# The expert program of a fused attention and MoE kernel starts one attention step sooner, and its 32-token unit moves from ninth to fifth place

## The chip, the cores and the metric

The kernel runs on one core of a Trainium2 chip. The metric is the device time of one execution in microseconds. The kernel before takes 522.33 us, the median of three runs (521.17, 522.33 and 524.80).

TensorE (PE) multiplies and turns matrices; VectorE (DVE) and ScalarE (ACT) work on elements; GpSimd (POOL) issues the indirect DMAs; SyncE (SP) issues the plain DMAs and the transposing ones.

## The reference

Block-sparse attention, then a mixture of experts with one expert per token (top 1):

```
batch, heads, seq, dim = 4, 8, 768, 64        # attention
scores = q @ k^T / sqrt(64), masked to neighbour blocks of 32, the first and last block,
         and 3 sampled blocks for each block
x = softmax(scores) @ v                       # as 3072 tokens x 512
logits = x @ w_gate                           # 512 x 8
e = argmax(logits); gate = softmax(logits)[e]; eom = sigmoid(x @ w_output_gate)[e]
out = gate * eom * (relu(x @ w1[e]) @ w2[e])  # w1: 512 x 1024, w2: 1024 x 512, of 8 experts
```

## The kernel before, in words

**Attention** runs in 52 steps (`NSTEP`), two halves of the batch by 4 dense and 22 sparse ones. A step's parts go by name: `pS` multiplies q and k into a PSUM tile S, `dM` takes the row maximum (DVE, L506), `aE` the exps (ACT, L514), `pT` turns the probabilities (PE L463, copies L466 on ACT and L468 on DVE), `pO` multiplies by v (L531, L542) and `fin` divides. The parts of three steps are interleaved.

**Routing** goes along in hooks, `at(step, rank, function)`: `turn` turns a tile of 128 tokens (xp, L622, copied at L628), `route_p` multiplies by the gate weights (lp, L638), `route_s`, `route_a`, `route_r` (rp, L681 to L684) and `route_c` find each token's expert and its place among that expert's tokens. `route_d` scatters the tokens into a table `rows` in HBM, sorted by expert (POOL, L752). When the last tokens are counted, a plan is worked out (`plan`: some 45 small DVE operations, from L770 to L831, with one matmul `lb` on the tile `left` at L824). It gives the places `place_u` from which POOL then gathers x of every expert unit but the first (L896). The first unit, "unit 0", takes 512 tokens that are known to belong to one expert before the attention ends; it is turned on PE (xe, L911) and split on ACT and DVE (L915, L916).

**The experts** work in 13 units of tokens by 8 pieces of FF, numbered as steps 0 to 103 of the expert program. A piece is 512 KB of weights that SP loads (`load_w`, L887) into one of 14 buffers. As the products are in two halves of f16, ACT writes the high half of a piece (`w_h`, L970), DVE the low half (`w_l`, L974). Step s is a product h (12 matmuls, L996; h0, h1 ... in order), the relu and its split on ACT (`h_h`, L1005) and DVE (`h_l`, L1011); four steps later (`YL`) the product y follows (L1031). When a unit's y is complete, ACT scales it (`y_o`, L1041) and POOL scatters it to the output (`store_y`, L1049). x of a unit is gathered in `load_x`, split by `x_s` on ACT (L935) and DVE (L936), and turned by SP's transposing DMAs (`x_t`, L945). Unit 1 (`PEX`) is turned on PE instead (xgp, L953), and split by ACT L955 and DVE L956.

**What sets the order.** Each engine works in the order in which instructions are emitted. `program()` gives every expert instruction a step and a rank in it with `do(step, rank, f, a)`. `PACE` says which of the first expert steps are emitted at the end of the attention steps from `FIRST` = 51 on, `PLAN` and `PLAN0` where the planner's parts stand, `LW` and `WW` the first steps for weight loads and splits, `LEAD` (7) how many steps ahead of its product a piece is split. `WALK` gives the order of the units. Units hold, in that order, 512, 256, 352, 256, 288, 256, 256, 256, 256, 32, 192, 160 and 32 tokens. PSUM has banks of the pools psS (S tiles, large turns, two of a unit's y), psT (turned probabilities, h) and psO (O, a unit's third y); `late` in the route functions takes one of psS, otherwise psO.

Of the kernel before, what the change touches and what calls it, by code (L numbers as in the profile page):

```python
# [34 lines left out]
NRAW = 14  # L35
# [3 lines left out]
NPU, NIF = 4, 9  # L39
NR = len(CAPS)  # L40
PS = NPU + NR + NIF
IFS = (2, 3, 4)
WALK = [0, 4, 1, 5, 2, 6, 3, 7, 10, 8, 9, 11] + list(range(NPU + NR, PS))


def widths(c):

    return [128] * (c // 4) + ([32 * (c % 4)] if c % 4 else [])


SHAPE = [[128] * EM] + [widths(CAPS[w - NPU] if NPU <= w < NPU + NR else 8) for w in WALK]
MT = 3
# [8 lines left out]
LEAD = 7  # L61
# [15 lines left out]
FIRST = 51  # L77

WPRE = 44, 48, 52, 52, 53, 53, 54, 54
PACE = -1, -1, 1, 1, 2, 3  # L80

PLAN = 2, 3, 4
PLAN0 = 4
LW, WW = 4, 6

PH = {}
PEX = (1,)
XT = {1: 6}
XE = 51, 52
XG = 42, 43, 44, 45  # L90

# [36 lines left out]
def tile_kernel(ctx, tc, q, k, v, sampled, wg, wcat, out):  # L128
# [724 lines left out]
    NP = NUNIT * NFC  # L853
    toks = [sum(sh) for sh in SHAPE]
    per = [2 if t <= 256 else 1 for t in toks]

    def load_t(u):
        if u:
            assert len(scattered) == NT
        src = es[WALK[u - 1]:WALK[u - 1] + 1, 0:1] if u else eai  # L860
        _, r = nc.values_load_multi_w_load_instructions(src, engines=[ET.SP], min_val=0, max_val=E - 1)
# [31 lines left out]
    def gather_x(u, x, m):  # L893
        place_ = place_u[:, WALK[u - 1], m:m + 1] if u else place_0[:, m:m + 1]
        n = NT if u else RG[GE][1]
        i = nc.gpsimd.indirect_dma_start(  # L896
            x.bitcast(I32), None, rows, bass.IndirectOffsetOnAxis(ap=place_, axis=0)).ins
        after_scatters(i, n)
        if not u:
            tc.declare_no_dep(i, group="table", reason="rows of first tiles", keep=kept[:n])  # L900
            tc.add_to_no_dep_group("table", i)
# [81 lines left out]
    def bank_of(n):  # L983
        return n - n % per[n // 8]
# [82 lines left out]
    def at(n, rank, f, *a):  # L1067

        hooks.setdefault((n, rank), []).append((f, a))
# [36 lines left out]
    for bp in range(2):  # L1106
        o = PER * bp
        for r in range(RK):
            at(o + r if bp or not r else r + 2, 3, fixed, bp, r)
        if bp:  # L1110
            for r in range(RC):
                at(o + 2, 3, fixed_v, bp, r)
        for i in range(NPAIR):
            u0 = o + ND + 2 * i
            if bp or i > 1:
                at(u0 - 6, 1, load_q, bp, i)
            at(u0 - 3 if bp or i else u0 - 1, 3 if bp or i else 0, scale_q, bp, i)
            for kind, n, ns in KC:
                at(u0 - n, 3, gather_k, bp, i, kind, ns)
            at(u0 - 2, 3, window_k, bp, i)  # L1120
            if bp or i:
                at(u0 - 2, 1, window_v, bp, i)
            at(u0 - 1, 1, gather_v, bp, i, 0)
            at(u0, 1, gather_v, bp, i, 1)
        tiles = [NPAIR] + list(range(NPAIR))
        for n, i in enumerate(tiles):
            tt = 12 * bp + n

            r = o + ND + 1 + (2 * i + 2 if n else 0)
            at(r + 1, 2, turn, tt, r + 1 >= LATE_T, "act" if r + 1 < LATE_T else "dve")  # L1130
            at(r + 2, 0, route_p, tt, r + 2 >= LATE_T)
            at(r + 2, 1, route_s, tt)
            for g, (a, e) in enumerate(RG):
                if e == tt + 1:
                    t0 = r + 2
                    if e == NT:
                        at(t0, 3, part, route_a, 20, g)
                        at(t0 + 1, 0, route_r, g, True)
                        at(t0 + 1, 0, route_b, g)
                        at(t0 + 1, 1, mixed, g)  # L1140
                        for t in range(a, e):
                            at(t0 + 1, 3, route_d, t)
                        continue
                    if e == RG[-2][1]:
                        at(t0 + 1, 3, part, route_a, 20, g)
                        at(t0 + 2, 3, route_r, g, True)
                        at(t0 + 2, 3, route_b, g)
                        at(t0 + 2, 3, part, route_c, 20, g)
                        for t in range(a, e):
                            at(t0 + 2, 3, route_d, t)  # L1150
                        continue
                    for m, n_ in enumerate(PARTS[0]):
                        at(t0 + m, 3, part, route_a, n_, g)
                    at(t0 + 3, 0, route_r, g, t0 + 3 >= LATE_T)
                    at(t0 + 3, 0, route_b, g)
                    for m, n_ in enumerate(PARTS[1]):
                        at(t0 + 3 + m, 1, part, route_c, n_, g)
                    for t in range(a, e):
                        at(t0 + 5 + (t - a) * (1 if g else 2), 3, route_d, t)
                    if g == GE:  # L1160
                        for m in range(5):
                            at(t0 + 4 + m, 3, part, choose, 4, g)
                        at(t0 + 9, 3, load_t, 0)
# [3 lines left out]
        at(n, 3, turn_early, 2 * m)  # L1167
    for n in range(2):
        at(50 + 2 * n, 3, w_h, n)
        at(50 + 2 * n, 3, w_l, n)  # L1170
    for j, s in enumerate(WPRE):
        at(s, 3, load_w, j)

    done = set()

    def program(n0, n1):

        prog = {}

        def do(step, rank, f, a, hi=n1):  # L1180
            u = NFC if f in (load_w, w_h, w_l, p_h, p_y, h_h, h_l) else 1
            if n0 * u <= a < hi * u and (f, a) not in done:
                done.add((f, a))
                prog.setdefault(step, []).append((rank, len(prog[step]) if step in prog else 0, f, a))

        for i in range(3):
            do(PLAN[i], 8.5 if i == 2 else 12.5, plan, i)
        for u in range(NUNIT):
            t = 8 * u
            if u:  # L1190
                do(max(t - 20, LW), 0, load_t, u)
                do(max(t - 16, PLAN[2]), 8.6, load_x, u)
                do(max(t - (12 if u > 2 else 8), WW), 13, x_s, u)
            do(max(t - 6, WW if u else 0), 13, keep_t, u)
            do(XT.get(u, max(t - (11 if u > 2 else 6), WW)), 15, x_t, u)
            do(t + 8 + YL - (not u), 9.5 if not u else 12, y_o, u)
            do(t + 8 + YL + 1, 13, store_y, u)
        for n in range(NP):
            w = max(n - LEAD, WW + (n - 8) // 2) if n >= 8 else max(n - 2, 1)
            do(w, 12, w_h, n)  # L1200
            do(w, 12, w_l, n)
            if n >= 8:
                do(max(n - NRAW - LEAD + 1, LW + (n - 8) // 3), 14, load_w, n)
            do(PH.get(n, n), 8, p_h, n)
            do(n + YL, 9, p_y, n)
            b = per[n // 8]
            if n % b == b - 1:
                do(n + (n != 1), 10 if n != 1 else 16, h_h, bank_of(n))
                do(n + (n != 1), 11 if n != 1 else 16, h_l, bank_of(n))
        return prog  # L1210

    def emit(prog, upto):
        for step in sorted(k for k in prog if k < upto):
            for _, _, f, a in sorted(prog.pop(step), key=lambda z: z[:2]):
                if f is load_w and 10 <= a < NRAW + 8:
                    paced(tc, ET.SP, f, (a,))
                else:
                    f(a)


    done.update([(x_t, 0), (w_h, 0), (w_h, 1), (w_l, 0), (w_l, 1)])
    main = program(0, NSURE)

    def unit(n):
# [11 lines left out]
    for step in range(max(s for s, _ in hooks) + 1):  # L1236
# [45 lines left out]
        if step >= FIRST:  # L1282
            emit(main, PACE[step - FIRST])
    emit(main, 10 ** 6)
# [3 lines left out]
    def rest(n, k):  # L1288
        with tc.If(more > n):
            emit(program(1 + NR + n, 1 + NR + n + IFS[k]), 10 ** 6)  # L1290
            in_order(tc)
            if k + 1 < len(IFS):
                rest(n + IFS[k], k + 1)
# [63 lines left out]
```

## Time and profile before

| | |
|---|---|
| median of three runs | 522.33 us (521.17 to 524.80) |
| profiled execution | 522.23 us, its span 520.4 us |
| mean granted PE clock | 0.985 |
| busy: PE, DVE, ACT, POOL | 494.6 (95%), 347.7 (67%), 314.2 (60%), 231.3 us (44%) |
| HBM | 112.06 MB read, 12.85 MB written |

Times in the trace run from the start of the span. Attention and routing end, and the experts begin, between about 226 and 255 us. A number in brackets behind a row of a timeline is the time for which the engine was idle before it, with what ended that.

### The profile page before, as it was taken

What the parts mean: (1) busy time and instruction counts of PE and PEld (TensorE: products, weight loads), DVE (VectorE), ACT (ScalarE), POOL (GpSimd) and SP (SyncE); (2) the same over time, 40 slices, a digit from 0 to 9 for tenths busy, and PEclk for the clock granted to TensorE, in tenths of its full rate; (3) what the DMA queues carried; (4) which work ended last, traced back from release to release, by engine and by line L of the source; (5) the groups of instructions that cost most, each with busy time, mean ns of one, the idle gap of its engine ahead of it and who ended that gap; (6) DMA issues with size and microseconds to landing.
All of it is one profiled execution on the core that took longest, in us unless ns stands there. A gap on an engine that the chain in (4) does not pass through costs nothing.

```text
span 520.4 us, 18358 instructions
## 1 busy us (share of the span) xinstructions
PE 494.6 (95%) x7405; PEld 337.6 (65%) x7405; DVE 347.7 (67%) x683; ACT 314.2 (60%) x558; POOL 231.3 (44%) x411
## 2 busy tenths in 40 slices
PE   8999999999999999988899999999999999997994
PEld 7767777776677677764346655666566666665662
DVE  5776678656878687668858555464656656668770
ACT  3566777665657677664346746365465656667661
POOL 7575565570458768714440616050323304336222
PEclk9999999999989999999999999999999999997998
DMA  7977788694978879839499999989969899799501
GB/s 293 302 246 231 239 269 283 212 304 155 247 213 260 273 223 291 257 120 293 170 379 354 339 321 379 270 206 327 256 224 243 286 283 275 230 353 309 154 30 37
DMA packets 59902, 131.88 MB, mean 253 GB/s; under 512 B 28320, under 2 KB 28448, under 8 KB 59810
## 3 DMA queue, kind: packets, MB, share of 16 engines
q1 hardware_dynamic: 47314, 86.84, 55.9%
q0 software_dynamic: 12496, 43.79, 25.5%
q8 instruction: 60, 0.98, 0.8%
q14 instruction: 32, 0.26, 0.2%
HBM read 112.06 MB, written 12.85 MB: 240 GB/s over the span
## 4 chain that ended last, share of the span: by engine, by line
PE 75%; issue 7%; DMA 5%; DVE 4%; POOL 4%; POOLq 2%; ACT 2%; ACTq 0%; DVEq 0%
PE y L1031 25%; PE h L996 24%; PE S L499 7%; PE T L463 6%; PE O L542 4%; PE O L531 4%; DMA vt<-in_v_dram,vidx 3%; PE xp L622 2%; PE lp L638 2%; POOLq L424 2%; POOL kr L433 1%; DVE kr L974 1%; DMA vq<-in_v_dram 1%; DMA r<-in_wcat_dram 1%; DMA raw<-in_sampled_dram 1%
## 5 line engine op out<-in xcount | busy, mean ns | idle before, releaser
L974 DVE SCALAR_TENSOR_TENSOR kr<-r,kr 128x1024 f16<-128x1024 f32 x80 | 97.3, 1223 | 59.0 <-ACT kr L970 58.9
L1031 PE MATMUL y<-kr,hh 128*128 128x512 f16 (+3 forms) x759 | 110.7, 313 | 0.0
L970 ACT ACTIVATE kr<-r 128x1024 f16<-128x1024 f32 x80 | 84.0, 1057 | 40.1 <-PE y L1031 39.7
L1049 POOL DMA_INDIRECT out_dram<-yo,tab x28 | 34.7, 1241 | 165.0 <-ACT yo L1041 160.5
L996 PEld LDWEIGHTS <-kr 128*128 128x128 f16 x960 | 78.1, 98 | 36.9 <-issue 5.8
L1031 PEld LDWEIGHTS <-hh 128*128 128x128 f16 (+3 forms) x984 | 61.4, 98 | 58.4 <-issue 11.1
L996 PE MATMUL h<-xall,kr 128*128 128x256 f16 (+5 forms) x864 | 90.2, 252 | 3.4 <-DVE hh L1011 3.4
L514 ACT ACTIVATE P<-S,mx 128x256 f32<-128x256 f32 x176 | 69.7, 492 | 6.8 <-DVE mx L506 6.8
L448 POOL DMA_INDIRECT vt<-in_v_dram,vidx x44 | 43.3, 984 | 64.5 <-PE O L542 43.1
L506 DVE TENSOR_REDUCE mx<-S 128x4 f32<-128x1024 f32 x44 | 53.7, 1221 | 25.5 <-PE S L499 13.1
L1005 ACT ACTIVATE hh<-h 128x512 f16<-128x512 f32 (+5 forms) x64 | 31.5, 493 | 49.2 <-PE y L1031 27.3
L433 POOL COPY kr<-kn 128x256 f32 x132 | 48.6, 409 | 9.7 <-issue 8.3
L466 ACT COPY pt<-T 128x512 f32<-128x512 f32 x66 | 36.7, 592 | 25.7 <-PE T L463 25.7
L499 PE MATMUL S<-kr,qall 64*32 64x256 f32 x1408 | 50.5, 383 | 1.5 <-issue 1.5
L463 PE MATMUL T<-ident,P 128*128 128x128 f32 x352 | 48.3, 280 | 0.3 <-issue 0.3
L1011 DVE SCALAR_TENSOR_TENSOR hh<-h,hh 128x512 f16<-128x512 f32 (+5 forms) x64 | 35.5, 555 | 17.8 <-ACT hh L1005 17.8
L974 DVE SCALAR_TENSOR_TENSOR wx<-r,wx 128x1024 f16<-128x1024 f32 x24 | 29.3, 1226 | 18.9 <-ACT wx L970 18.9
L463 PEld LDWEIGHTS T<-ident,P 128*128 128x128 f32 x352 | 39.5, 143 | 3.2 <-issue 0.6
L896 POOL DMA_INDIRECT xb<-rows,place_u x24 | 32.9, 1370 | 12.0 <-issue 5.8
L996 PE MATMUL h<-xall,wx 128*128 128x256 f16 (+4 forms) x288 | 36.5, 279 | 0.0
L1031 PE MATMUL y<-wx,hh 128*128 128x512 f16 (+3 forms) x225 | 36.1, 321 | 0.0
L752 POOL DMA_INDIRECT rows<-xall,place x24 | 25.0, 1043 | 22.3 <-DVE xall L714 15.2
(271 smaller groups left out, 691.0 us busy)
## 6 DMA issues: line engine op xcount, KB each, us to landing
r<-in_wcat_dram SPq DMA_DIRECT2D x104, 512.0 KB, 5.7
vq<-in_v_dram SPq DMA_DIRECT2D x8, 780.0 KB, 4.8
qall<-in_q_dram SPq DMA_DIRECT2D x24, 256.0 KB, 5.2
vcall<-in_v_dram SPq DMA_DIRECT2D x22, 260.0 KB, 4.0
kn<-in_k_dram SPq DMA_DIRECT2D x10, 384.0 KB, 5.6
kn<-in_k_dram SPq DMA_DIRECT2D x3, 768.0 KB, 8.5
vcall<-in_v_dram SPq DMA_DIRECT2D x12, 130.0 KB, 10.5
vt<-in_v_dram,vidx POOLq DMA_INDIRECT x44, 6.2
```

Source lines behind the costliest of these rows:

```text
L433: nc.gpsimd.tensor_copy(r[:, slot], kn[bp][:, :, ds(rv, 1)].rearrange("p u o n -> p u (o n)"))
L448: nc.gpsimd.indirect_dma_start(vt[bp, i][:, s].rearrange("p b j w -> p (b j w)"), None, v, bass.IndirectOffsetOnAxis(ap=vidx[:, bp, i, s:s ...
L463: nc.tensor.transpose(pt[:, 128 * c:128 * c + 128], p[:, 128 * c:128 * c + 128], ident)
L466: nc.scalar.copy(t[:, 0:w], pt[:, 0:w])
L499: nc.tensor.matmul(s[64 * b + 32 * qi:64 * b + 32 * qi + 32, h2, hp], t[p, 64 * j + 32 * qi:64 * j + 32 * qi + 32], g[p, 1 - qi:3:1 + qi, ...
L506: nc.vector.tensor_reduce(mx, self.s.rearrange("p b h n -> p (b h) n"), axis=AX.X, op=ALU.max, negate=True)
L514: nc.scalar.activation(p[:, 256 * hp:256 * hp + 256], self.s[:, b, hp], AF.Exp, bias=self.mx[:, 2 * b + hp:2 * b + hp + 1])
L970: nc.scalar.activation(w[:, 0, r], piece(n // 8, n % 8)[:, r], AF.Copy, scale=SW)
L974: nc.vector.scalar_tensor_tensor(w[:, 1, r], piece(n // 8, n % 8)[:, r], SW, w[:, 0, r], op0=ALU.mult, op1=ALU.subtract)
L996: nc.tensor.matmul(hps[g][:, cols(n)], w[:, hl, 128 * c:128 * c + 128], x[:, xl, c, 0:t], start=cnt == 0, stop=cnt == 11)
L1011: nc.vector.scalar_tensor_tensor(hl[:, k], hps.pop(g)[:, k], 0.0, hh[:, k], op0=ALU.max, op1=ALU.subtract)
L1031: nc.tensor.matmul(y[t * p:t * p + t, 0:d], a[:, k:k + t], w[:, l, 512 + d * p:512 + d * p + d], start=n % 8 == 0 and cnt == 0, stop=n % 8 ...
```

## The change

Five things, of which none changes what is computed.

- `WALK`: the unit of 32 tokens that stood ninth stands fifth. Units now hold 512, 256, 352, 256, 288, 32, 256, 256, 256, 256, 192, 160 and 32 tokens.
- `PACE`, `PLAN`, `LW`, the step of `load_t` and `XT`: the expert steps 1 and on are emitted one attention step sooner; the plan, the loads of weights and of x keep their places by standing one expert step later. x of unit 1 is turned behind h7, between two products, rather than behind y2.
- `route_r` of the last group but one takes a bank of psO.
- The low split of piece 0 is emitted at step 51, behind the row maximum.
- `split_steps` gives the step at which each piece is split: instead of seven steps ahead throughout, it adds up for each step the time that its product takes against that of one split, puts splits off where steps are too short for them, and catches up. The loads follow the splits.

```diff
-WALK = [0, 4, 1, 5, 2, 6, 3, 7, 10, 8, 9, 11] + list(range(NPU + NR, PS))
+WALK = [0, 4, 1, 5, 10, 2, 6, 3, 7, 8, 9, 11] + list(range(NPU + NR, PS))
...
-PACE = -1, -1, 1, 1, 2, 3
+PACE = -1, -1, 1, 2, 3, 4
-PLAN = 2, 3, 4
+PLAN = 3, 4, 5
-LW, WW = 4, 6
+LW, WW = 5, 6
-XT = {1: 6}
+XT = {1: 7}
...
-                        at(t0 + 2, 3, route_r, g, True)
+                        at(t0 + 2, 3, route_r, g, False)
...
-        at(50 + 2 * n, 3, w_l, n)
+        at(50 + 2 * n + (not n), 3 - (not n), w_l, n)
...
+    def split_steps():
+
+        at_, n, idle = {}, 8, 1.4
+        for step in range(8):
+            at_[step] = max(step - 2, 1)
+        for step in range(NP):
+            t = toks[step // 8]
+            idle = min(idle + max(t * 0.0102, 0.68) - 0.1 - t * 0.00115, 2.4)
+            while n < NP and n <= step + LEAD and step >= WW + (n - 8) // 2 and (idle >= 0 or n <= step + 1):
+                at_[n] = step
+                idle -= 1.2
+                n += 1
+        return at_
+
+    split = split_steps()
...
-                do(max(t - 20, LW), 0, load_t, u)
+                do(max(t - 20, PLAN[1] + 1), 0, load_t, u)
...
-            do(XT.get(u, max(t - (11 if u > 2 else 6), WW)), 15, x_t, u)
+            do(XT.get(u, max(t - (11 if u > 2 else 6), WW)), 8.5 if u in XT else 15, x_t, u)
...
-            w = max(n - LEAD, WW + (n - 8) // 2) if n >= 8 else max(n - 2, 1)
+            w = split[n]
...
-                do(max(n - NRAW - LEAD + 1, LW + (n - 8) // 3), 14, load_w, n)
+                do(max(split[n - NRAW] + 1 if n >= NRAW else 0, LW + (n - 8) // 3), 14, load_w, n)
```

DVE at attention step 51: `mx_1_10_1` is that step's row maximum, `kr2_208` at L974 the low half of weight piece 0, `lsum` and `den` small routing and softmax operations, `pt1` the copy of turned probabilities. One piece of the difference, the change with + and the kernel before with -:

```order
+L506 TENSOR_REDUCE mx_1_10_1_6076<-S_1_10_1_6025 128x4
+L642 COPY lsum_212<-lp21_6042 128x16
+L475 TENSOR_SCALAR den_1_9_1_6079<-O_1_9_1_6051 128x4
+L476 RECIPROCAL den_1_9_1_6079<-den_1_9_1_6079 128x4
+L477 TENSOR_TENSOR xall_209<-O_1_9_1_6051,den_1_9_1_6079 128x2x128
 L974 SCALAR_TENSOR_TENSOR kr2_208<-r0_5410,kr2_208 128x1024
-L506 TENSOR_REDUCE mx_1_10_1_6077<-S_1_10_1_6026 128x4
-L642 COPY lsum_212<-lp21_6043 128x16
-L475 TENSOR_SCALAR den_1_9_1_6080<-O_1_9_1_6052 128x4
-L476 RECIPROCAL den_1_9_1_6080<-den_1_9_1_6080 128x4
-L477 TENSOR_TENSOR xall_209<-O_1_9_1_6052,den_1_9_1_6080 128x2x128
 L468 COPY pt1_1_10_0_6096<-T1_1_10_0_6091 128x512
```

The maximum and four small operations pass ahead of the split.

PE at the handover, from the first expert product to the second y; a product's other matmuls and weight loads are left out. Before:

```order
L996 MATMUL h0_6278<-qall_211,kr2_208 128x512
...
L622 MATMUL xp23_6296<-ident_76,xall_209 128x128 x4
L638 MATMUL lp23_6305<-wst_183,xT23_6295 64x16 x8
...
L996 MATMUL h1_6332<-qall_211,kr2_208 128x512
...
L770 MATMUL cp_6365<-cum5_218,ones_86 128x8
...
L996 MATMUL h2_6388<-qall_211,kr2_208 128x512
...
L996 MATMUL h4_6480<-qall_211,kr0_206 128x512
...
L824 MATMUL lb_6493<-left_6448,ones_86 128x42
...
L1031 MATMUL y0_6507<-kr2_208,hh0_6345 128x512
...
L996 MATMUL h5_6531<-qall_211,kr0_206 128x512
...
L1031 MATMUL y0_6507<-kr2_208,hh1_6352 128x512
```

And now:

```order
L996 MATMUL h0_6278<-qall_211,kr2_208 128x512
...
L622 MATMUL xp23_6296<-ident_76,xall_209 128x128 x4
...
L996 MATMUL h1_6305<-qall_211,kr2_208 128x512
...
L638 MATMUL lp23_6328<-wst_183,xT23_6295 64x16 x8
...
L996 MATMUL h2_6355<-qall_211,kr2_208 128x512
...
L770 MATMUL cp_6380<-cum5_218,ones_86 128x8
...
L996 MATMUL h4_6427<-qall_211,kr0_206 128x512
...
L1031 MATMUL y0_6440<-kr2_208,hh0_6318 128x512
...
L996 MATMUL h5_6513<-qall_211,kr0_206 128x512
...
L824 MATMUL lb_6526<-left_6481,ones_86 128x42
...
L1031 MATMUL y0_6440<-kr2_208,hh1_6325 128x512
```

One product stands between the last turn (xp23) and its use (lp23) where none stood, and the first y and the sixth h stand ahead of the planner's matmul `lb`.

ACT behind the last steps of the unit that precedes the 32-token unit's end: `yo` is that unit's y_o, `wx` and `kr` are splits, `vcall` is x_s, and the next `hh` is that of the small unit's third pair of steps, with whose low half (L1011) the PSUM bank comes free that the next unit's first h takes. Before (yo8 is the 256-token unit ahead of it):

```order
L1005 ACTIVATE hh74_8732<-h74_8642 128x64
L1041 ACTIVATE yo8_0_8735<-y8_8500,gate8_8235 128x512
L1041 ACTIVATE yo8_1_8737<-y8_8500,gate8_8235 128x512
L970 ACTIVATE wx_99<-r8_6527 128x1024
L935 ACTIVATE vcall_210<-xb2_6503 128x2x512
L970 ACTIVATE kr2_208<-r0_5410 128x1024
L1005 ACTIVATE hh76_8804<-h76_8706 128x64
```

And now (yo4 is the 288-token unit):

```order
L1005 ACTIVATE hh42_7861<-h42_7753 128x64
L1041 ACTIVATE yo4_0_7864<-y4_7530,gate4_7245 128x512
L1041 ACTIVATE yo4_1_7866<-y4_7530,gate4_7245 128x512
L1041 ACTIVATE yo4_2_7868<-y4_2_7531,gate4_7245 128x128
L970 ACTIVATE kr2_208<-r8_6557 128x1024
L935 ACTIVATE vcall_210<-xb1_6533 128x2x512
L1005 ACTIVATE hh44_7935<-h44_7835 128x64
```

A third tile of y_o stands ahead of the next `hh`, and one split instead of two.

## Rows read from the trace of the kernel before

**Rows 1.** Windows: stretch, length, busy (count) of each engine, PEclk, DMA share, GB/s

```profile
226.00:255.00 29.00, 22.48 (x253) 13.50 (x251) 24.82 (x91) 13.65 (x23) 8.18 (x10) 1.00 0.53 181
274.00:464.00 190.00, 190.00 (x1351) 121.34 (x1350) 116.84 (x122) 112.61 (x141) 55.99 (x60) 1.00 0.97 287
472.00:478.00 6.00, 6.00 (x57) 4.72 (x56) 5.12 (x7) 3.59 (x5) 4.47 (x6) 0.50 1.21 256
146.00:151.00 5.00, 4.49 (x71) 3.81 (x76) 2.38 (x11) 1.60 (x3) 2.62 (x4) 0.66 0.59 169
```

**Rows 2.** Timeline of PE, 222 to 300 us: start, length, instruction, idle before

```profile
222.66 1.09 PE L499 MATMUL S<-kr,qall 64*32 64x256 f32 x32
...
236.31 0.17 PE L681 MATMUL rp<-oh,tri 128*128 128x8 f16 x1 [1.02 <-DVE qall L916]
...
239.40 0.60 PE L622 MATMUL xp<-ident,xall 128*128 128x128 f32 x4
240.78 0.65 PE L638 MATMUL lp<-wst,xT 128*64 128x16 f32 x16 [0.78 <-DVE xT L628]
...
250.49 2.75 PE L996 MATMUL h<-qall,kr 128*128 128x512 f16 x12 [0.57 <-DVE hh L1011]
254.78 0.19 PE L824 MATMUL lb<-left,ones 21*128 21x42 f16 x1 [1.54 <-DVE left L818]
...
260.10 2.75 PE L1031 MATMUL y<-kr,hh 128*128 128x512 f16 x12
...
273.92 1.47 PE L996 MATMUL h<-xall,kr 128*128 128x256 f16 x12
...
299.94 1.95 PE L996 MATMUL h<-xall,kr 128*128 128x352 f16 x12
```

**Rows 3.** Timeline of DVE, 226 to 236 us

```profile
226.02 1.23 DVE L974 SCALAR_TENSOR_TENSOR kr<-r,kr 128x1024 f16<-128x1024 f32 x1 [3.69 <-ACT kr L970]
227.16 1.22 DVE L506 TENSOR_REDUCE mx<-S 128x4 f32<-128x1024 f32 x1
...
235.04 1.22 DVE L916 SCALAR_TENSOR_TENSOR qall<-xe,qall 128x1024 f16<-128x1024 f32 x1
```

**Rows 4.** Timeline of PE, 465 to 481 us

```profile
465.60 0.45 PE L996 MATMUL h<-xall,kr 128*128 128x32 f16 x12
...
468.02 0.35 PE L1031 MATMUL y<-kr,hh 128*32 128x128 f16 x12
471.78 2.08 PE L996 MATMUL h<-xall,kr 128*128 128x192 f16 x12 [3.40 <-DVE hh L1011]
...
478.67 1.16 PE L996 MATMUL h<-xall,wx 128*128 128x192 f16 x12
...
480.04 1.16 PE L996 MATMUL h<-xall,kr 128*128 128x192 f16 x12
```

**Rows 5.** Timeline of ACT, 465 to 469 us

```profile
465.85 1.27 ACT L1041 ACTIVATE yo<-y,gate 128x512 f32<-128x512 f32 x2 [0.48 <-issue]
467.01 1.05 ACT L970 ACTIVATE wx<-r 128x1024 f16<-128x1024 f32 x1
467.96 1.05 ACT L935 ACTIVATE vcall<-xb 128x1024 f16<-128x1024 f32 x1
```

**Rows 6.** Timeline of DVE, 470 to 472 us

```profile
470.38 1.22 DVE L974 SCALAR_TENSOR_TENSOR kr<-r,kr 128x1024 f16<-128x1024 f32 x1
471.51 0.22 DVE L1011 SCALAR_TENSOR_TENSOR hh<-h,hh 128x64 f16<-128x64 f32 x1
```

**Rows 7.** Timeline of POOL at 265 us, when the first gathered x is there

```profile
264.74 0.99 POOL L870 COPY gate<-xb 128x2 f32<-128x2 f32 x1 [2.16 <-DMA xb<-rows,place_u]
```

**Rows 8.** Timeline of SP's queue, unit 2's three transposes

```profile
284.68 10.61 SPq L945 DMA_TRANSPOSE xall<-vcall  x3
```

**Rows 9.** DMA, 270 to 301 us

```profile
DMA packets 5961, 10.85 MB, mean 350 GB/s; under 512 B 3511, under 2 KB 3511, under 8 KB 5960
```

**Rows 10.** Timeline of PE at 147 us, ahead of the first half-clock stretch

```profile
146.82 1.08 PE L542 MATMUL O<-vt,pt 128*32 128x65 f32 x30 [0.52 <-DMA vt<-in_v_dram,vidx]
```

## Prediction

> **What bounds the kernel now.** I read the page first: PE is busy for 494.6 us, 95% of the 520.4 us span, and the next engine, DVE, for 67%. So time can come only from PE's idle gaps, from its work, or from its clock. The change leaves the work as it is (the same 7,927 PE instructions in another order), which leaves gaps and clock. Next I read PE by stretches. Through most of the expert part it never stops: 190.00 busy of 190.00 us, at the full clock [rows 1]. Of the gaps that the change can reach there are two. The first is the handover from attention and routing to the experts, 226 to 255 us: 22.48 busy of 29.00, so **6.52 us** idle [rows 1]. The second is the seam behind the 32-token unit, where PE waits 3.40 us [rows 4] and then runs at half clock (0.50, that is 1.2 GHz, for all of 472 to 478) [rows 1]. Three steps there take 6.89 us (471.78 to 478.67) where the next takes 1.37 (478.67 to 480.04) [rows 4], so the clock costs 6.89 - 3 x 1.37 = **2.8 us** and the seam 6.2 in all.
>
> The timelines say what each gap waits for. At the handover: DVE runs the first low split at 226.02 ahead of the last attention step's max (227.16) [rows 3], though PE finished S at 223.75 (222.66 + 1.09) [rows 2]; the exps and the transposes stand behind that max. Then PE waits 1.02 for L916 to let go of an S bank that `rp` is given, 0.78 for the turned x of the router, 0.57 for a low half of h, and 1.54 for the planner's `left` [rows 2]; what is left of the 6.52 are waits behind that max and shorter ones. At the seam ACT and DVE stand between PE and its next h: two y_o tiles, a split, the conversion of x [rows 5] and another split, and only then the small h_h; DVE likewise runs a split at 470.38 before its h_l at 471.51 [rows 6].
>
> **The change part by part: the handover.** Nothing is added here; the order of work changes, so I carry PE's time forward, wait by wait. (1) With the split behind it, mx of step 51 starts at 224.0, once S is there. That is 3.1 us sooner, but the split (1.23, and not before ACT has written its high half) and the small copies now stand between it and the DVE copy of the turned probabilities that PE needs; so of the 3.1 I count about 1.65 for all PE work behind it. (2) `rp3` now takes a bank of psO, so it no longer waits 1.02 for L916. The wait doesn't vanish: the second half of h0 reads what L916 writes. That DVE instruction, at 235.04 before [rows 3], comes 1.7 sooner and ends by about 234.5. h0 then ends at 236.95 where it ended at 239.40 [rows 2]: 2.45 gained. (3) h1 stands between the turn (xp23) and the router's product (lp23), so the 0.78 us lies under its 2.6 us. With part of the 0.57-us wait, h3 ends 3.7 us sooner. (4) y0 and h5 stand ahead of `lb`, whose `left` I expect at about 253.3; 1.54 us [rows 2] are covered by products that were ready. At 254.3 seven products (six h, one y) are done, a state PE had at 260.10 [rows 2]: 5.8 us. (5) x of unit 1 can't come sooner by as much: its gathers wait for the plan, which is only 0.6 us earlier, so the rows that POOL saw landed by 264.74 [rows 7] land at about 264.1. The turn `xgp` stands behind h7 at 264.7, so it does not wait. But its two conversions stand on ACT and DVE ahead of the halves of h6 and h7, and h8 waits about 0.5 us for them. h8, at 273.92 before [rows 2], starts at 268.7: 5.2 us.
>
> A second way to the same number: 6.52 us of idle less what I still see in the new order (0.66 at the exps, 0.37 for a low half, two of 0.2, 0.5 before h8, about 2.0 in all) leaves 4.5. I take **4.9**, bounds 4.5 to 5.2.
>
> Moved with it are DMAs. Weight loads from the ninth on keep their wall time, since they come one program step later in a program one step sooner. Unit 2's turn by three transposes on SP must now be in 5.2 us earlier: h16 stood at 299.94 without a wait [rows 2], now at about 294.7. SP issued the three from 284.68 in 10.61 us [rows 8], behind 28 weight loads; the planner now puts 25 ahead. In that time 350 GB/s were moved [rows 9], so 512 KB took about 1.5 us of the whole DMA, and three loads fewer are 4.5 us. Before, x was in by 299.94; by the loads alone it is in by 295.4, and the buffers that the loads wait for come free sooner too, with h. I expect no wait, or 0.7 at most, and put nothing for it; the uncertainty is in the rivals.
>
> **The seam.** WALK moves the 32-token unit from ninth to fifth, behind one of 288 tokens. PE arrives 2.75 us after that unit's last big y: four pairs of small h and y, as from 465.60 to 468.38 before [rows 4]. On ACT, from the same instant: 0.25 until the first y_o, 1.16 for two full tiles as before [rows 5], about 0.25 for the 32-row third, one split and x's high part (0.95 from one start to the next, as 467.01 to 467.96 [rows 5]), h_h. On DVE x's low part follows the split: 1.13 each (470.38 to 471.51 [rows 6]), then 0.27 for h_l and the handoff. That ends 5.30 us after the last big y, against 6.1 before, because one split fewer stands ahead. PE waits 5.30 - 2.75 = 2.55, and about 0.2 at the next step: 2.7 where it was 3.4.
>
> What the clock then does, no row shows. The price lies between 0 (it stays) and 2.8 (it falls as long as before). The trace has a nearer row than the seam: over 146 to 151 us the clock is 0.66, so it stood at half for about 3.4 of the 5 us [rows 1], and the longest wait just before was 0.52 us [rows 10]. So a wait of 2.55 amid thin products is more likely to cost the clock than not. I take 1.7, half of those 3.4 us. The seam then costs 4.4, a gain of **1.8** (bounds 0.7 and 3.5). The Trainium skill ("TensorE: Matmul & The Clock Gate", section "Why this matters for your kernels") ties a drop to idle gaps between bursts of matmuls, and would by that spare a kernel whose gap shrinks (513.7); the row with 0.52 us disagrees, so I give its reading a rival's chance only.
>
> The planner of splits also puts off splits inside the small unit. PE there needs a piece each 0.7 us while ACT gives one per 0.95 and DVE one per 1.13, so stock is drawn down; I count at least four pieces left, and the conversions that were put off fall in the 256-token steps, 2.6 us long, where ACT and DVE were 59 to 61% busy (112.61 and 116.84 of 190.00) [rows 1]. Cost: nothing. Were that cover gone, one DVE split, 1.14, would show at each late step.
>
> **Sum.** 522.23 (the profiled run; the median of the three is 522.33) - 4.9 - 1.8 = 515.5. I say 515.4.
>
> **Rivals.** *The clock stays up* at the new seam: the seam costs 2.7, and the time is 515.5 - 1.7 = 513.7. For it: a shorter wait than 3.40. Against: the 0.52-us row. 0.27. *Unit 2's x lands somewhat late*, at 295 to 298.6: POOL's stores and gathers use the same DMA engines, which are 0.97 busy there [rows 1]. h16 waits 0.5 to 4: 516 to 519.5. 0.15. *The seam gives nothing* (the change doesn't do there what it says: another split or a late load ahead of x): 3.4 + 2.8 as before, and 517.3. 0.08. *Slower*: the transposes don't move at all, since loads saved ahead of them are replaced by later loads and gathers that share the engines; they land up to 299.9, h16 waits from 294.7, 5.2 us, and the gap costs the clock, 2.8 more: 515.5 + 8.0 = 523.5. It decides from a landing at about 298.6, where wait and clock eat the 6.7 gained. Against: three loads' bytes are truly out of the way. 0.05. My forecast keeps 0.45.
>
> **Numbers.** A difference under 1%, 5.2 us, can't be told from none here (the three runs lie 3.6 apart), so faster means below 517.1. The forecast and the first rival lie below, though the bounds of the terms (4.5 + 0.7) reach 517.0; the second is half on each side; the third and fourth within 1%. With some small chance for a stall that I did not see: faster 0.69, within 1% 0.25, slower 0.06. The range takes the first rival and its better bounds (522.2 - 5.2 - 3.5 = 513.5, and a clock dip less elsewhere) down to 512.3, and most of the second up to 519.5.
>
> **What would show it.** PE idle from 226 to 255 near 2 us instead of 6.52; `lb` without a wait; h8 near 268.7; h16 without a wait for a transpose; at the seam behind the fifth unit a wait of about 2.6 for h_l, and a clock of 1.00 or 0.50 after it; none behind the old place. A wait before h16, a wait of PE on a split in units 5 to 7, or a half-clock stretch inside 226 to 290 would make the prediction wrong.

## The result and the profile after

The changed kernel took 520.6 us, the median of 20 executions (511.61 to 528.14), and the kernel before 523.06 beside it (519.25 to 530.29). The ratio is **0.9859, with a 95% interval of 0.9821 to 0.9897**, so by this ratio it is faster by 1.4%; times 523.06 that is 515.7, where 515.4 was forecast. The ratio keeps only executions within 1.5% of each kernel's fastest, 6 of the 20 against 18 of the 20 before, so it flatters the change: the plain medians lie 0.5% apart. Two more measurements, on two chips, gave 519.65 against 522.37 (0.9887, 0.9844 to 0.9931) and 518.04 against 523.89 (0.9885, 0.9818 to 0.9951), so 1.1% by the ratio, and 0.5 and 1.1% by the medians.

The profiled execution took 511.61 us, the fastest of the 20; it must not be read as typical. The lines of the page that answer to the table of before:

```profile
span 509.8 us, 18354 instructions
PE 490.6 (96%) x7405; PEld 333.4 (65%) x7405; DVE 346.6 (68%) x683; ACT 314.0 (62%) x558; POOL 231.1 (45%) x411
PEclk9999999999999999999999999999999999999998
```

First the two ends of the stretch that the change touches. The last S of the attention starts at 218.03; before, it started at 222.66 [rows 2]. Up to there no engine's order has changed, and in fourteen profiled executions of nine kernels it stands anywhere from 218.0 to 225.5. So 4.6 of the 10.6 us between the two spans are not the change's, and I count from the last S on.

PE of the changed kernel, 218 to 292 us (start, length, instruction, idle before):

```profile
218.03 1.09 PE L499 MATMUL S<-kr,qall 64*32 64x256 f32 x32
...
229.87 2.54 PE L996 MATMUL h<-qall,kr 128*128 128x512 f16 x11 [0.20 <-DVE qall L916]
232.24 0.60 PE L622 MATMUL xp<-ident,xall 128*128 128x128 f32 x4
...
235.36 0.65 PE L638 MATMUL lp<-wst,xT 128*64 128x16 f32 x16
...
241.86 2.75 PE L996 MATMUL h<-qall,kr 128*128 128x512 f16 x12 [0.41 <-DVE hh L1011]
...
249.72 0.19 PE L824 MATMUL lb<-left,ones 21*128 21x42 f16 x1
249.84 2.76 PE L1031 MATMUL y<-kr,hh 128*128 128x512 f16 x12
...
260.21 1.04 PE L953 MATMUL xgp<-ident,xb 128*128 128x128 f32 x8
...
264.22 1.47 PE L996 MATMUL h<-xall,kr 128*128 128x256 f16 x12 [0.38 <-DVE hh L1011]
...
291.93 1.95 PE L996 MATMUL h<-xall,kr 128*128 128x352 f16 x12 [1.54 <-DMA xall<-vcall]
```

The waits of 0.78 and 1.54 [rows 2] are gone: `lp` and `lb` carry no bracket. Of the 1.02 for L916, 0.20 is left, inside h0. From the last S to h8 it is 46.19 us, before 51.26: **5.07 gained**. But h16, without a wait before, now waits 1.54 for a transpose of x.

Windows (stretch, length, busy of PE, PEld, DVE, ACT, POOL, PEclk, DMA share, GB/s): the handover, shifted by the 4.63 us of the last S, and the new seam.

```profile
221.37:250.37 29.00, 27.75 (x279) 15.98 (x277) 25.41 (x91) 15.24 (x25) 9.95 (x10) 1.00 0.49 182
379.00:385.00 6.00, 5.85 (x57) 4.04 (x57) 6.00 (x8) 4.55 (x6) 3.40 (x4) 0.72 1.19 196
```

Idle at the handover is 1.25 us instead of 6.52 [rows 1]. The seam on PE, ACT and DVE:

```profile
376.66 0.35 PE L1031 MATMUL y<-kr,hh 128*32 128x128 f16 x12
379.15 1.91 PE L996 MATMUL h<-xall,kr 128*128 128x256 f16 x12 [2.14 <-DVE hh L1011]
380.99 0.51 PE L1031 MATMUL y<-kr,hh 128*32 128x128 f16 x12
381.43 2.45 PE L996 MATMUL h<-xall,kr 128*128 128x256 f16 x12
```

```profile
374.10 1.52 ACT L1041 ACTIVATE yo<-y,gate 128x512 f32<-128x512 f32 x3 [1.13 <-PE y L1031]
375.50 1.06 ACT L970 ACTIVATE kr<-r 128x1024 f16<-128x1024 f32 x1
376.45 1.06 ACT L935 ACTIVATE vcall<-xb 128x1024 f16<-128x1024 f32 x1
377.40 0.23 ACT L1005 ACTIVATE hh<-h 128x64 f16<-128x64 f32 x1
```

```profile
376.60 1.22 DVE L974 SCALAR_TENSOR_TENSOR kr<-r,kr 128x1024 f16<-128x1024 f32 x1 [3.38 <-ACT kr L970]
377.74 1.22 DVE L936 SCALAR_TENSOR_TENSOR vcall<-xb,vcall 128x1024 f16<-128x1024 f32 x1
378.88 0.21 DVE L1011 SCALAR_TENSOR_TENSOR hh<-h,hh 128x64 f16<-128x64 f32 x1
```

The reader sees the row of work that the prediction drew up: three y_o, one split, x, h_h; on DVE split, x, h_l. PE waits 2.14 where it waited 3.40 [rows 4]. The clock is 0.72 in the window: part of it at half (1.2 GHz), less than the 0.50 throughout of before [rows 1].

From the last S to the end it is 291.8 us, before 297.8: 6.0 us, of which +5.07 at the handover, -1.7 up to h16, +2.6 behind it.

### The profile page after: what moved, and what is told of

Same layout as the page of the kernel before. It is cut to its first block, busy times and chain, and to the rows that moved or that the text cites. A ratio compares the mean times of both kernels' runs of the same rounds, so it can differ in the third digit from the quotient of the medians.

```text
span 509.8 us, 18354 instructions
## 1 busy us (share of the span) xinstructions
PE 490.6 (96%) x7405; PEld 333.4 (65%) x7405; DVE 346.6 (68%) x683; ACT 314.0 (62%) x558; POOL 231.1 (45%) x411
## 4 chain that ended last, share of the span: by engine, by line
PE 72%; DMA 7%; issue 7%; DVE 5%; SPq 2%; POOL 2%; ACT 2%; POOLq 2%; ACTq 0%; DVEq 0%
PE y L1031 22%; PE h L996 22%; PE S L499 7%; PE T L463 6%; PE O L542 4%; PE O L531 4%; PE xp L622 2%; PE lp L638 2%; DMA kn<-in_k_dram 2%; DMA r<-in_wcat_dram 2%; SPq L945 1%; DMA xall<-vcall 1%; DMA vt<-in_v_dram,vidx 1%; POOLq L424 1%; POOL kr L433 1%
## 5 line engine op out<-in xcount | busy, mean ns | idle before, releaser
L974 DVE SCALAR_TENSOR_TENSOR kr<-r,kr 128x1024 f16<-128x1024 f32 x80 | 97.3, 1223 | 55.5 <-ACT kr L970 53.8
L1031 PE MATMUL y<-kr,hh 128*128 128x512 f16 (+3 forms) x741 | 113.9, 318 | 0.0
L996 PEld LDWEIGHTS <-kr 128*128 128x128 f16 x960 | 80.3, 98 | 38.5 <-issue 7.7
L1031 PEld LDWEIGHTS <-hh 128*128 128x128 f16 (+3 forms) x984 | 61.2, 98 | 58.2 <-issue 10.6
L996 PE MATMUL h<-xall,kr 128*128 128x256 f16 (+5 forms) x864 | 93.7, 257 | 4.1 <-DVE hh L1011 2.5
L1011 DVE SCALAR_TENSOR_TENSOR hh<-h,hh 128x512 f16<-128x512 f32 (+5 forms) x64 | 35.5, 555 | 15.9 <-ACT hh L1005 15.9
L974 DVE SCALAR_TENSOR_TENSOR wx<-r,wx 128x1024 f16<-128x1024 f32 x24 | 29.1, 1223 | 16.1 <-ACT wx L970 16.1
L752 POOL DMA_INDIRECT rows<-xall,place x24 | 26.9, 1121 | 19.1 <-DVE xall L714 13.4
L531 PE MATMUL O<-vcall,pt 128*64 128x65 f32 x704 | 31.0, 227 | 2.2 <-issue 0.8
L970 ACT ACTIVATE wx<-r 128x1024 f16<-128x1024 f32 x24 | 25.1, 1056 | 12.9 <-PE y L1031 12.2
```

The source lines that it names most:

```text
L531: nc.tensor.matmul(o[64 * b:64 * b + 64, h2, hp, 0:VW], t[:, col:col + 64], cv[:, h2, 4 * b + 2 * hg + hp], start=h2 == 0 and hp == 0, sto ...
L970: nc.scalar.activation(w[:, 0, r], piece(n // 8, n % 8)[:, r], AF.Copy, scale=SW)
L974: nc.vector.scalar_tensor_tensor(w[:, 1, r], piece(n // 8, n % 8)[:, r], SW, w[:, 0, r], op0=ALU.mult, op1=ALU.subtract)
L996: nc.tensor.matmul(hps[g][:, cols(n)], w[:, hl, 128 * c:128 * c + 128], x[:, xl, c, 0:t], start=cnt == 0, stop=cnt == 11)
L1031: nc.tensor.matmul(y[t * p:t * p + t, 0:d], a[:, k:k + t], w[:, l, 512 + d * p:512 + d * p + d], start=n % 8 == 0 and cnt == 0, stop=n % 8 ...
```

## The experiments

Each kernel was timed in five rounds against the kernel before on the same chip, but for a single execution that is told as such. Where several are compared from trace to trace, this table has what the text uses. It is worked out from PE's timelines: starts of the last S, h8, h16, h48 and h56.

| kernel | last S to h8 | h8 to h16 | wait before h16 | wait at seam | h48 to h56 |
|---|---|---|---|---|---|
| before | 51.26 | 26.02 | 0 | 3.40 (ninth) | |
| changed | 46.19 | 27.71 | 1.54 | 2.14 | 18.77 |
| changed, again | 46.17 | 27.81 | 1.63 | 2.1 | 19.87 |
| changed, third time | 46.17 | 27.95 | 1.8 | 2.14 | 17.21 |
| changed, fourth time | 46.18 | 29.56 | 3.38 | 2.1 | 18.76 |
| handover alone | 46.17 | 33.47 | 7.30 | 3.40 (ninth) | |
| seam alone | 52.20 | 27.53 | 1.34 | 2.1 | 17.21 |
| earlier transposes | 46.17 | 26.01 | 0 | 2.1 | 19.87 |
| the same, again | 46.03 | 26.02 | 0 | 2.1 | 18.77 |

**The changed kernel again**, no edit.

> The changed kernel once more, as the measure for the variants beside it and to tell what of the profiled 10.4 us (522.23 to 511.61) belongs to the change. Theory A (the change gives 5 us at the handover and 2 at the seam, loses 1.5 before h16, and the 4.6 us of difference that lie before 221 us are the spread of the attention part): ratio to the kernel before 0.985 to 0.99; in the trace h8 stands 38 to 39.5 us behind the O product of attention step 50 whatever the attention took, and h16 waits 1 to 3 us for a transpose. Rival B (the attention part is faster by the change too): ratio 0.98 or below, and the attention again ends about 4 us sooner.

519.65 us, ratio 0.9887 (0.9844 to 0.9931); 518.79 in the profile. One of the 12 executions took 1201 us; no profile shows why. The last S starts at 223.94, and h8 stands 46.17 us behind it, as in the first profile to 0.02. So the handover's gain is the change's, and the early end of the attention in the first profile was not (rival B falls). h16 waits 1.63.

**The handover alone.**

```diff
 # kernel before, with the changed PACE, PLAN, LW, XT, load_t, route_r, place of w_l(0), rank of x_t(1)
 WALK = [0, 4, 1, 5, 2, 6, 3, 7, 10, 8, 9, 11] + ...    # as before
 w = max(n - LEAD, WW + (n - 8) // 2) ...               # as before
```

> The kernel before with the edits of the handover alone (expert program one step sooner, turn of x behind h7, bank of rp3, low split behind the maximum); order of units and splits as before. Theory A: PE idle from the last O to h8 falls by 5 us as in the changed kernel; but 28 weight loads stand ahead of unit 2's transposes, so h16 waits longer for them, 3 to 6 us, and the seam of 6 us stays: ratio 0.993 to 1.0. Rival C (the number of loads ahead does not set when the transposes land; other traffic does): h16 waits 1 to 2 as in the changed kernel and the ratio is 0.99 to 0.993.

520.85 us, ratio 0.9934 (0.9891 to 0.9977). h8 gains its 5.1 us, and then h16 waits:

```profile
299.33 3.09 PE L996 MATMUL h<-xall,kr 128*128 128x352 f16 x10 [7.30 <-DMA xall<-vcall]
```

That h runs at half clock, and so does what follows (the columns are those of the windows above):

```profile
299.30:303.70 4.40, 4.37 (x15) 2.14 (x16) 0.15 (x1) 0.46 (x1) 0.00 (x0) 0.50 1.05 415
```

From h16 to h24 it takes 29.46 us instead of 27.27, so the clock costs 2.2 more. Here the whole gain of the handover is given back 30 us later, in this execution more than all of it; the ratio, a gain of 0.7%, suggests that others lose less. Theory A's sign is right and its size too small (3 to 6 expected). Its reason is wrong, as SP's rows show:

```profile
212.37 64.98 SPq L887 DMA_DIRECT2D r<-in_wcat_dram  x25
277.65 13.26 SPq L945 DMA_TRANSPOSE xall<-vcall  x3
```

25 loads stand ahead of the transposes, as in the changed kernel (x25 there, too), and not 28: `LW = 5`, an edit of the handover, takes the three away, and not the planner, as the prediction had it. The two kernels run the same instructions in the same order on every engine from 30 us to 309 us, past h16. So 7.30 here and 1.54 there are the same work in two executions. Rival C is right in that the number of loads doesn't decide, and its 1 to 2 us are too few here.

**The seam alone.**

```diff
 # changed kernel, with PACE, PLAN, LW, XT, load_t, route_r, place of w_l(0), rank of x_t(1) as before
```

> The kernel before with the new order of units and the new steps of the splits alone; handover as before. Theory A: idle at the handover 6 to 7 us as before; no wait before h16; behind the 32-token unit a wait of 2.0 to 2.6 us and a granted clock at half for 0 to 4 us, and no gap at the old place; ratio 0.995 to 0.998. Rival D (the seam's move gives nothing, the clock's cost is as before): ratio 1.0.

519.85 us, ratio 0.9964 (0.9927 to 1.0). The wait at the seam is 2.1, and h48 to h56 takes 17.21, the least of all. What theory A did not expect is a wait before h16 here, too:

```profile
301.19 1.95 PE L996 MATMUL h<-xall,kr 128*128 128x352 f16 x12 [1.34 <-DVE hh L1011]
```

```profile
299.58 0.68 DVE L1011 SCALAR_TENSOR_TENSOR hh<-h,hh 128x512 f16<-128x512 f32 x1
```

The row names h_l, but that ended at 300.26, 0.93 us ahead of h16; the semaphore that the last transpose raises is complete at 301.10 in this trace, so it was x. The name in such a bracket must be held against the time of its end. SP has 28 loads ahead of the transposes here, as in the kernel before:

```profile
213.37 69.81 SPq L887 DMA_DIRECT2D r<-in_wcat_dram  x28
```

From 30 us to 319 us this kernel runs the same instructions in the same order on every engine as the kernel before, where x had landed at 299.01, 0.93 us ahead of h16 [rows 2]. So the kernel before comes close to this wait, and the same work shows it in another execution. (The table's 52.20 has a stretch at half clock in it: the granted clock is 0.50 from 230 to 233 us here.)

**Transposes one step sooner.**

```diff
-            do(XT.get(u, max(t - (11 if u > 2 else 6), WW)), 8.5 if u in XT else 15, x_t, u)
+            do(XT.get(u, max(t - (11 if u > 2 else 7), WW)), 8.5 if u in XT else 15, x_t, u)
```

> The changed kernel with unit 2's three transposes one expert step sooner on SP, ahead of the last three weight loads before them. Theory A (they were late because of what is queued ahead): they land 3 us sooner, h16 waits 0 to 0.3 us, and the time is 1 to 2 us below that of the changed kernel beside it. Rival E (they wait for the converted x or share the DMA engines with loads in flight, whatever stands ahead): they land less than 1 us sooner and the time is the same.

512.59 us (511.94 to 514.46), ratio 0.98 (0.9766 to 0.9835). h16 does not wait. SP's rows, the changed kernel first, then this one:

```profile
276.85 10.37 SPq L945 DMA_TRANSPOSE xall<-vcall  x3
```

```profile
277.41 8.71 SPq L945 DMA_TRANSPOSE xall<-vcall  x3
```

Counted from h8, the three are issued at 9.77 us instead of 12.63, and take 8.71 us instead of 10.37 (before: 10.76 us behind h8 and 10.61 [rows 2, 8]). So the changed kernel issued them 1.9 us later against h8 than the kernel before; the prediction had them in by 295.4 with h8 5.2 sooner, 0.7 later against h8 at most. Theory A holds in the trace, and in the time by more than it said: 7.1 us below the changed kernel beside it.

**The same one edit in the kernel before.**

```diff
-            do(XT.get(u, max(t - (11 if u > 2 else 6), WW)), 15, x_t, u)
+            do(XT.get(u, max(t - (11 if u > 2 else 7), WW)), 15, x_t, u)
```

> The kernel before with one edit: unit 2's three transposes one expert step sooner, ahead of three weight loads. Theory F (in many executions of the kernel before, too, x of unit 2 lands after h16 is due, though the profiled one showed no wait; this is what spreads its times): its executions lie closer together than 519.5 to 530.7, and the median falls by 2 to 4 us, ratio 0.993 to 0.996. Rival G (the kernel before has no such wait, the spread is of the attention part): same spread, ratio 1.0.

523.53 us, ratio 0.9986 (0.9953 to 1.0018): nothing. Theory F falls: the wait that the seam alone shows is too rare or too small in the kernel before to move its median, and the edit is worth something only once h16 comes 5 us sooner.

**y_o behind the small unit's relus.** Scaling the 288-token unit's y moves four steps on, with its store; transposes sooner as above.

```diff
-            do(t + 8 + YL - (not u), 9.5 if not u else 12, y_o, u)
-            do(t + 8 + YL + 1, 13, store_y, u)
+            do(t + 8 + YL - (not u) + 4 * (u == 4), 9.5 if not u else 12, y_o, u)
+            do(t + 8 + YL + 1 + 4 * (u == 4), 13, store_y, u)
```

> The changed kernel with the transposes of unit 2 one step sooner, and the three y_o of the 288-token unit four expert steps later (behind the relu of the small unit's last pair), with their store. Theory A (at the seam ACT and DVE stand between PE and its next h, and y_o's 1.4 us of ACT is the piece that the small steps can't cover): the wait of 2.1 us falls to 0.3 or less, the clock stays at 1.00 there, and the time is 2 to 4.5 us below the variant with the transposes alone, 508 to 510.5. Rival H (the next thing is late at once: the splits that now start no sooner, or DVE): a wait of 1 to 2 us stays, on a split or on h_l, and the time falls by under 1 us.

511.63 us, ratio 0.9768 (0.9722 to 0.9814). PE of this kernel at the seam, then the window behind it:

```profile
380.14 0.35 PE L1031 MATMUL y<-kr,hh 128*32 128x128 f16 x12
380.42 1.48 PE L996 MATMUL h<-xall,kr 128*128 128x256 f16 x12
...
388.15 1.47 PE L996 MATMUL h<-xall,kr 128*128 128x256 f16 x12 [0.87 <-DVE hh L1011]
```

```profile
380.00:386.00 6.00, 6.00 (x98) 4.53 (x95) 4.50 (x5) 5.81 (x10) 4.07 (x5) 1.00 1.18 261
```

The 2.14 is gone and the clock stays at 1.00 (2.4 GHz). But the work behind y_o comes due four steps later: ACT splits four pieces in a row (381.76 to 385.67), DVE the same four (382.86 to 387.49), and h_l stands behind them, so 0.87 us of wait comes back, and the time misses the 508 to 510.5 of theory A. So y_o was what the small steps couldn't cover, and a part of rival H is true as well: something else is late next.

**Two edits of the handover undone** (transposes sooner as above).

```diff
-                        at(t0 + 2, 3, route_r, g, False)
+                        at(t0 + 2, 3, route_r, g, True)
...
-        at(50 + 2 * n + (not n), 3 - (not n), w_l, n)
+        at(50 + 2 * n, 3, w_l, n)
```

> The changed kernel with the transposes one step sooner, and two small edits of the handover undone: the low split of piece 0 ahead of the last row maximum again, and rp3 in a bank of psS. Theory A (they gave the first 2.45 us of the handover): h0 ends 2 to 2.5 us later against the last S, h8 1 to 2.5 us later; the time is 1 to 2.5 us above the variant with the transposes alone. Rival I (the plan or the landing of x limits h8, so that these two are hidden): h8 and the time the same within 0.5 us.

517.42 us, ratio 0.9887 (0.9849 to 0.9925). The 1.02-us wait is back, and h8 stands 48.44 us behind the last S, 2.27 later than with the two edits:

```profile
236.98 0.17 PE L681 MATMUL rp<-oh,tri 128*128 128x8 f16 x1 [1.02 <-DVE qall L916]
```

Theory A: the two are worth 2.3 of the 5.1 us in the trace. In time they can't be told so well: the variant with both was measured on other chips, at ratios of 0.98 and 0.985, which is 1.9 to 4.5 us.

**Splits seven steps ahead again** from piece 32 on (transposes sooner as above).

```diff
+        for n in range(32, NP):
+            at_[n] = max(n - LEAD, WW + (n - 8) // 2)
         return at_
```

> The changed kernel with the transposes one step sooner, and from piece 32 on the splits seven steps ahead throughout, as before (loads with them). Theory A (by putting splits off the planner took one split out of the way at the seam): the wait behind the 32-token unit is 3.0 to 3.6 us instead of 2.1, and the time 1 to 2 us above the variant with the transposes alone. Rival J (the planner does nothing measurable): wait within 0.3 us of 2.1, same time.

516.07 us, ratio 0.9837 (0.9793 to 0.9882). The seam's wait is that of before again, and the step behind it runs at the lower clock (2.72 us long, against 1.47 at the full one):

```profile
386.06 2.72 PE L996 MATMUL h<-xall,kr 128*128 128x256 f16 x12 [3.28 <-DVE hh L1011]
```

So without the planner the move of the unit gains no wait; the split that it puts off is the 1.1 us, and rival J falls in the trace. The time shows no difference that I would claim (0.98 and 0.985 with the planner, on other chips).

**The changed kernel, a third time.**

> The changed kernel again. Open: its median is 519 to 521 us, but the two profiled executions (511.61 and 518.79) wait only 1.5 and 1.6 us before h16, while the variant with earlier transposes runs 7 us faster. Theory K (the lateness of unit 2's x differs from execution to execution, 1 to 8 us, and half-clock stretches follow it): an execution at 519 us or more shows a wait of 3 us or more before h16, or a half-clock stretch behind it. Rival L (what differs is the attention part and the clock at the seam): the wait is again 1.3 to 1.8, and from the last S to the end the profile has 291 to 294 us whatever its total.

518.04 us, ratio 0.9885 (0.9818 to 0.9951). The profiled execution (513.77) waits 1.8, and takes 290.4 from the last S to the end, near what rival L said. Theory K spoke of executions of 519 us or more, and this was none.

**The changed kernel, a fourth time**, one execution.

> One more look at the changed kernel. Theory K: another wait before h16 than in the looks before, beyond 1.3 to 1.8 us. Rival L: 1.3 to 1.8 us again, and 291 to 294 us from the last S to the end.

515.97 us, and the wait is another, as theory K said; from the last S to the end it takes 293.6, as rival L said:

```profile
296.33 1.95 PE L996 MATMUL h<-xall,kr 128*128 128x352 f16 x12 [3.38 <-DMA xall<-vcall]
```

**Earlier transposes again.**

> The variant with unit 2's transposes one step sooner again, beside the changed kernel on one chip. Theory K: it stays 5 to 8 us below the changed kernel beside it, its executions lie within 4 us of each other, and h16 does not wait. Rival L: its lead was chance; it is 1.5 to 3 us below, and its times spread as those of the others.

514.38 us (512.02 to 518.7), ratio 0.985 (0.9796 to 0.9904): 3.7 us below the changed kernel beside it, half of the lead of before and with a wider spread, between what theory K (5 to 8) and rival L (1.5 to 3) said. No wait before h16.

**Late y_o again.**

> The variant that also puts the y_o of the 288-token unit behind the small unit's relus, again, beside the others on one chip. If the seam's wait (0.9 where it was 2.1) and the clock that doesn't fall are worth what the trace shows, it is 1 to 4 us below the variant with the transposes alone; if the seam's clock loss is rare, within 1 us of it.

511.31 us, ratio **0.9767 (0.9713 to 0.9821)**: the same as in the first measurement, 3.1 us below the variant beside it and 6.7 below the changed kernel. This version beats both kernels.

Theory K (a lateness that differs between executions) is borne out by 1.5, 1.6, 1.8 and 3.4 us in four traces of one kernel, and by 7.3 with 2.2 of clock behind it in the kernel with the handover alone, which does the same work up to there. Rival L holds for most of what the four totals differ by: their last S starts between 218.0 and 223.9, and from there to the end they take 290.4 to 293.6. All four took 511.6 to 518.8 us, none the 520 to 528 that nearly half of the kernel's executions take. For those only the granted clock is on record: 0.984 in the mean of the 16 of 520 us or more, 0.990 in that of the 22 shorter ones (0.993 to 0.996 in the twelve with late y_o). I estimate from the unrounded difference, 0.0055 of 518 us, that the clock makes 2.9 us of the 7.0 by which the long ones are longer. Where they lose it, and what the other 4 us are, no trace shows; so of the 3.7 to 7.1 us that earlier transposes gave, the traces of the changed kernel account for 1.5 to 3.4.

## Why the prediction came out as it did

**The handover was right, by its steps.** Counted from the last S: PE's work behind the maximum comes 1.8 sooner (`lp22` at 9.07 us, before 10.88; 1.65 said). h0 ends 2.53 sooner (2.45 said). h3 ends some 3.8 sooner (3.7 said). y1 stands 5.6 sooner (5.8 said). `lb` waits for nothing. h8 waits 0.38 for the low half queued behind xgp's conversions (0.5 said), and comes 5.07 sooner (4.9 taken, 4.5 to 5.2 given). The two ways to the number agreed within their bounds, and walking the waits forward was the nearer one.

**The seam was right in kind and a little small.** h_l ended at 379.09, 4.9 us behind the last big y (374.23), where I had 5.30: y_o begins at 374.10, about as that y ends, where I gave a hand-off of 0.25. The three y_o take 1.40 until the split, as said (1.41). The wait is 2.14 (2.55 said). For the clock I took 1.7 of 0 to 2.8. Eight executions of the same 2.1-us wait show the eight steps from h48 in 17.21 us (three times), 18.77 (three) and 19.87 (twice): a loss of 0, 1.56 and 2.66, mean 1.25. So both the forecast and its first rival happen, to the same instructions, from one execution to the next. Two windows, the changed kernel's third profile first, then its second:

```profile
382.80:388.80 6.00, 5.88 (x80) 4.50 (x80) 6.00 (x8) 6.00 (x8) 3.37 (x4) 1.00 1.06 187
```

```profile
385.00:391.00 6.00, 5.86 (x44) 3.60 (x47) 5.92 (x7) 3.46 (x4) 3.38 (x4) 0.51 1.03 173
```

The gain in the first profile is 6.2 - 2.14 - 1.56 = 2.5, where 1.8 was said. But the 2.8 for the old seam was one execution, too: behind the same 3.40-us wait, the three steps that took 6.89 us take 5.38 in the kernel before with earlier transposes and 6.15 with the handover alone, so the clock cost 2.8, 1.3 and 2.0 there. In the mean the old seam costs 5.4 and the new one 3.4. The 1.8 is near that difference of 2.0 because both prices, 6.2 and 4.4, were too high, by 0.8 and 1.0; that is luck.

**The step that failed is unit 2's x**: "I expect no wait, or 0.7 at most". It waited 1.54, 1.63, 1.8 and 3.38. The working took three loads fewer ahead of the transposes for 4.5 us, as if the queue were a pipe that is always full. The trace shows them issued only 3.2 us sooner against the last S (58.82 instead of 62.02 us), and the last one landed 2.6 sooner, while h16 was due some 5 us sooner and had 0.93 us to spare before. SP's loads wait for PE (total, times, longest; before and changed):

```profile
SPq L887 <- PE y L1031: 14.1, 5, 4.3
```

```profile
SPq L887 <- PE y L1031: 14.3, 5, 4.1
```

The last of these five waits ends 55.35 us behind the last S before and 54.18 in the changed kernel, as these loads keep their wall time, which the prediction itself says. Behind it SP issues nine loads before and six now, in 6.67 and 4.64 us. So 1.2 + 2.0 us is the whole gain: three loads are worth the time of their issue, 2.0 us, and not the 4.5 us of their bytes. Nor does the number of loads decide: with 25 ahead the wait was 1.5 to 7.3 us, with 28 it was 0 and 1.3. What lets the same work land up to 5.8 us apart (27.6 to 33.3 us behind h8 in five profiles) stays open. This is the second rival, "lands somewhat late", which had 0.15; it came beside the forecast's gains, not in their place, and its price here, 1.5 to 3.4, lies inside its 0.5 to 4. The slower rival, transposes that don't move and the clock's price behind the wait, is what the handover alone met: 7.30 and 2.2, where 5.2 and 2.8 were said. In the changed kernel it did not come, in the executions seen.

**The sum.** 5.1 + 2.5 - 1.7 = 5.9 in the first profile against 6.7 said, and 515.7 by the ratio against 515.4. The terms that were too small and the one that was left out partly cancel, so the agreement is closer than the working deserves. It also hangs on the ratio: the plain median, 520.6, lies above the whole range that was given (512.3 to 519.5). The 7,927 PE instructions of the prediction stand in no view; the page counts 7405 matmuls before and after, so that the work is unchanged is right. And the profiled run that I started from, 522.23, was taken as the fixed point, though its attention part alone can differ by several us between executions.

The Trainium skill ("TensorE: Matmul & The Clock Gate", section "Why this matters for your kernels") ties a drop of the clock to idle gaps. The runs agree in part: without the gap (late y_o) the clock stayed up in the window shown, and with one and the same gap of 2.14 us, shorter than those the page warns of, it fell five times and stayed three. So the gap alone doesn't decide; whether it is needed, two profiles without it don't show.

## What to carry to other kernels

When work is moved earlier, list every transfer that feeds it and ask when that transfer can *start*, not how many bytes stand ahead of it: 5 us won at the handover were partly lost 25 us later to three transposes, and moving their issue by one step took that wait away. In an engine's queue, work whose result nobody awaits (y_o) should stand behind the short conversions that PE waits for. And compare traces from a common event, here the last S: the spans of two profiles differ by things that the change does not touch.

## What the runs showed of the hardware

The attention part, with its instructions in the same order, ended anywhere from 218.0 to 225.5 us (start of the last S, fourteen profiles); among what varies are waits for gathered v (0.2 to 2.7 us at a time) and, in some executions, stretches at the lower clock. The granted clock behind a wait of 2.1 us was 1.00, 0.72 or 0.51 in the same kernel (windows of 6 us), so such a loss can't be told from one profile. Issuing unit 2's three transposes took 7.95 to 13.26 us (fourteen profiles), and 10.27 to 13.26 in the five whose order up to there is the changed kernel's.
